# One block of rows, and one product per token tile, for two groups of remainder channels in the X accumulation of a layer's backward pass

## The chip, the cores and the metric

The kernel runs on one core of a Trainium2 chip. The metric is the time of one execution on the device in microseconds. Three runs of the kernel before took 1150.02, 1150.79 and 1152.15 us; their median is 1150.79 us. The engines are named as in the profile: PE (TensorE's products), PEld (its weight loads), DVE (VectorE), ACT (ScalarE), POOL (GpSimd) and SP (SyncE, whose queue issues nearly all DMAs).

## The reference

The program computes a layer's output and all its gradients. The layer has a global branch (self-attention over T = 4000 tokens, one head of D = 144 channels) and a local branch (a gated convolution of width 5), both fed from the layer norm of x; a second convolution and a product merge them. B is 2.

```python
xa = _layernorm(x)
q, k, v = split(xa @ w_qkv)
p = softmax(q @ k.T * D ** -0.5)
glob = (p @ v) @ w_att_out
h = gelu(xa @ w_mlp_in)                 # 2 D channels
u, g = h[..., :D], _layernorm(h[..., D:])
loc = (u * conv5(g, dw_csgu)) @ w_mlp_out
m = concat(glob, loc)
out = x + (m + conv5(m, dw_merge)) @ w_merge
# and the gradients of x and of the seven weights for a given grad_out
```

The gradient with respect to xa is what matters here. It has three parts for a token: one from the keys and values (sums over all query tiles), one from the queries, and one from the local branch's first product, whose input gradient has 2 D = 288 channels.

## The kernel before

Tokens are laid out as 125 partitions by 32 blocks per batch, so a token tile is 125 tokens, and there are 64 tiles in two batches. A channel dimension of 144 is one block of 128 and a remainder of 16; the 288 channels of the inner gradient are two blocks of 128 and a remainder of 32.

`phase_att` walks through 64 query tiles in steps. In step s it computes, for 32 key blocks at a time, the scores of tile s (`quad`, lines 1187 and 1194), their row minimum (`S_min`, 1209), exponentials (`P_exp`, 1215), and the product of probabilities and their gradient (`PdP`, 1225 and 1226). The results lie in Pbuf and Sbuf; DMA transposes issued by SP turn them into PT and ST (1219 and 1405). `Y_half` (1236) multiplies PT with xa, `Z_half` (1266) ST with xa. Y gives the row sums, the scalars rl, delta and nd (1242 to 1245), and yn, a copy for later (1247) that goes to memory (1248). Z becomes a row zn of 144 channels (1270): the query part of the gradient before its weight M1T. zn lies in columns 512 to 767 of a buffer qb, whose first 512 columns hold the q rows of a later tile; one DMA transpose per tile (`jit_tr`, 1165) turns all of it, so Z's transposed form is two blocks of 128: channels 0 to 127, and the 16 remaining with zeros behind them.

`X_group` adds up the gradient of xa in PSUM for up to three token blocks (1322) and adds it to acc in SBUF (1329). For each block its products are: one from Sbuf and one from Pbuf for every query tile of the group; two with M1T from Z's transposed blocks; and three with WiT from the inner gradient's blocks. The latter come from `local_units`: the local branch runs in 16 pairs of tiles per batch beside attention, `e_dh` writes the inner gradient into dhr (687), columns 0 to 287 of 384, and `dhT_unit` has it transposed (691).

The order of the instructions on each engine is not the program's: `Planner.ORDER` holds one list for each of PE, DVE, ACT, POOL and SP, and `plan` ties each instruction to the one before it in the list. SP's list orders the DMA issues. POOL has mostly the addition that makes the second row of QBs (1256), the powers for the layer norms (600), l_w (681) and additions to accumulators (698).

Before the loop, `Head` makes the weights of the products: `m1t` M1T, `conv` WiT by transposing w_mlp_in on PE and copying on ACT (298 to 301). After it, `Merge` and `Final` compute the outputs.

Of the kernel before, what the change touches and what calls it, by code (L numbers as in the profile page):

```python
# [120 lines left out]
class Head:  # L121
# [84 lines left out]

    def m1t(self):
        self.fused(self.WkT, self.WqT, float(D) ** -0.5, self.W.M1T)
# [81 lines left out]
    def conv(self):  # L290
# [10 lines left out]
        nc.scalar.copy(W.WiT[0:32, 2, :], pt[0:32, 2, :])  # L301
        nc.sync.dma_start(W.Wc[:, 0, :], k.dw_csgu.rearrange("k c -> (k c)").partition_broadcast(128))
# [35 lines left out]
def pre_pieces(k, W, b, S, pst):  # L338
# [4 lines left out]
    if True:  # L343
# [20 lines left out]
        def ln_mv(g):  # L364
# [9 lines left out]
            nc.gpsimd.tensor_tensor(S.rstd_x[:, sl], veps[:, sl], k.mhalf[0:PB, sl], op=ALU.pow)  # L374
# [42 lines left out]
def prep_late(k, W, b, S, es, pst):  # L417
# [7 lines left out]
    st = one([PB, NB, 6], F32, "pst")  # L425
# [26 lines left out]
    def stats(g):  # L452
        sl = slice(8 * g, 8 * g + 8)
        for j in range(8):
            nc.vector.bn_stats(st[:, 8 * g + j, :], xin[:, 8 * g + j, :])
        ma, mb, va, vb = st[:, sl, 1], st[:, sl, 4], st[:, sl, 2], st[:, sl, 5]
        nc.vector.tensor_tensor(dm[:, sl], ma, mb, op=ALU.subtract)
        nc.vector.tensor_tensor(sm[:, sl], ma, mb, op=ALU.add)
        nc.vector.tensor_tensor(veps[:, sl], va, vb, op=ALU.add)
        nc.vector.scalar_tensor_tensor(dm[:, sl], dm[:, sl], 0.25 * D, dm[:, sl], op0=ALU.mult, op1=ALU.mult)  # L460
        nc.vector.tensor_tensor(veps[:, sl], veps[:, sl], dm[:, sl], op=ALU.add)
        nc.vector.tensor_scalar(veps[:, sl], veps[:, sl], 1.0 / D, EPS, op0=ALU.mult, op1=ALU.add)
        nc.gpsimd.tensor_tensor(S.rstd_x[:, sl], veps[:, sl], k.mhalf[0:PB, sl], op=ALU.pow)
# [53 lines left out]

G2 = 2
# [5 lines left out]
def local_units(k, W, b, S, A, es, DHT, ps_w, gw):  # L524
# [6 lines left out]
    sm = es.enter_context(tc.tile_pool(name="loc_sm%d" % b, bufs=4, side=side, reuse_waits="tile"))  # L531
# [30 lines left out]
    def slot(g):  # L562
        return g % 3
# [119 lines left out]
    def e_dh(g):  # L683
# [3 lines left out]
        nc.vector.tensor_tensor(dhr[g % 2][0:PB, :, 0:2 * D], dd[:], gpr[slot(g)][:], op=ALU.mult)  # L687

    def dhT_unit(g):
        dhT = gw.tile([128, 3 * G2, 128], BF, tag="dhT", bufs=3)  # L690
        nc.sync.dma_start_transpose(out=dhT[:], in_=dhr[g % 2][:].rearrange("p a b -> p (a b)"))
        for bi in range(G2):
            DHT[G2 * g + bi] = [dhT[:, 3 * bi + ct, :] for ct in range(3)]
# [82 lines left out]
class Planner:  # L776

    ORDER = {
# [1414 lines left out]
```

## Time and profile before

| | us |
|---|---|
| median of three runs | 1150.79 |
| profiled execution | 1152.39 |
| its span | 1150.5 |
| PE busy in the span | 1118.8 |
| DVE busy | 1021.0 |
| ACT busy | 906.5 |
| POOL busy | 249.5 |

A row of a group gives line, engine, operation, the tile written and those read, the shapes and the count; then busy us, mean ns of one instruction, idle time of the engine just before, and what ended it. Successive matmuls overlap, so their mean duration is longer than their spacing. A row of the timeline gives start, length, engine, line, operation and tiles; for SP it is the issue of a DMA, not its landing. SPq, ACTq and so on are the engines' sequencers.

### The profile page before, as it was taken

The page shows a single profiled execution, that of the slowest core. Times are in us where ns is not written, and L with a number is a line of the kernel's source. Part 1 is how long each engine was busy: PE and PEld are TensorE (multiplying, and loading weights), DVE is VectorE, ACT ScalarE, POOL GpSimd, SP SyncE. Part 2 cuts the span into 40 slices and gives each one's busy share as a digit, 9 for nine tenths or more (in the row PEclk, how much of TensorE's full clock was granted, in tenths as well). Part 3 has the DMA queues.
Part 4 walks back from the last instruction along what each step waited for, and adds up shares of the span by engine and source line. Part 5 has one row for each costly group of instructions (what it writes and reads, how often), then busy time and mean ns, then how long its engine had stood idle before and what let it go on. Part 6 is the DMA issues. An engine that isn't in the chain of part 4 may idle for free.

```text
span 1150.5 us, 35851 instructions
## 1 busy us (share of the span) xinstructions
PE 1118.8 (97%) x14293; PEld 868.7 (76%) x14293; DVE 1021.0 (89%) x3063; ACT 906.5 (79%) x1641; POOL 249.5 (22%) x427
## 2 busy tenths in 40 slices
PE   6999999999999999999999999999999999999998
PEld 3667777777777677777777777777777777699987
DVE  8699999999999998877999999999999997667656
ACT  5999898899898767777989889888889877615372
POOL 8111112111121113431001111111111112013642
PEclk9999999999999999999999999999999999999999
DMA  4688887979988989998988989888888899978973
GB/s 117 155 160 176 173 181 158 192 159 173 174 166 159 188 181 182 201 187 183 207 183 178 171 158 168 161 181 152 173 174 154 187 177 183 224 173 219 245 144 101
DMA packets 680887, 200.72 MB, mean 174 GB/s; under 512 B 657815, under 2 KB 674093, under 8 KB 680699
## 3 DMA queue, kind: packets, MB, share of 16 engines
q1 hardware_dynamic: 678352, 194.69, 84.6%
q0 software_dynamic: 2192, 3.62, 1.1%
q8 instruction: 111, 1.82, 0.7%
q14 instruction: 56, 0.46, 0.1%
q10 hardware_dynamic: 176, 0.12, 0.0%
HBM read 24.62 MB, written 18.01 MB: 37 GB/s over the span
## 4 chain that ended last, share of the span: by engine, by line
PE 64%; DMA 13%; DVE 11%; ACT 7%; issue 2%; SPq 1%; POOL 1%; ACTq 0%; DVEq 0%; POOLq 0%
PE X L1322 18%; PE ps L1187 14%; PE yz L1236 8%; PE yz L1266 8%; PE ps L1194 5%; DMA PT<-Pbuf 5%; DVE Pbuf L1209 4%; ACT Pbuf L1215 3%; PE po L1708 2%; DMA ST<-Sbuf 2%; PE pd L610 1%; DVE Sbuf L1226 1%; PE pj L1147 1%; ACT Sbuf L1225 1%; DMA go_h<-in_grad_out_dram 1%
## 5 line engine op out<-in xcount | busy, mean ns | idle before, releaser
L1209 DVE TENSOR_SCALAR_CACHE_REDUCE Pbuf<-ps 125x1000 bf16<-125x1000 f32 x256 | 306.2, 1197 | 30.1 <-PE ps L1194 22.4
L1225 ACT CAST Sbuf<-ps 125x1000 bf16<-125x1000 f32 x249 | 248.7, 999 | 86.7 <-PE ps L1194 66.2
L1215 ACT ACTIVATE Pbuf<-Pbuf,nm 125x1000 bf16<-125x1000 bf16 x256 | 284.9, 1144 | 4.4 <-DVE nm L1211 4.2
L1322 PE MATMUL X<-QBs,Pbuf 125*128 125x144 bf16 x2048 | 281.1, 226 | 0.2 <-POOL QBs L1256 0.2
L1322 PE MATMUL X<-QBs,Sbuf 125*128 125x144 bf16 x2048 | 281.3, 226 | 0.0
L1187 PE MATMUL ps<-xaT_m,qt 128*128 128x500 bf16 x1024 | 260.6, 374 | 5.0 <-DVE Pbuf L1209 3.5
L1322 PEld LDWEIGHTS <-Sbuf 125*128 125x128 bf16 x2048 | 198.2, 98 | 18.8 <-issue 18.5
L1322 PEld LDWEIGHTS <-Pbuf 125*128 125x128 bf16 x2048 | 200.2, 98 | 1.3 <-issue 1.1
L1226 DVE TENSOR_TENSOR Sbuf<-Sbuf,Pbuf 125x1024 bf16<-125x1024 bf16 x249 | 170.8, 690 | 7.9 <-ACT Sbuf L1225 6.0
L1236 PE MATMUL yz<-xa_aug,PT 125*128 125x145 bf16 x2048 | 151.0, 227 | 6.5 <-DMA PT<-Pbuf 6.4
L1266 PE MATMUL yz<-xa_aug,ST 125*128 125x144 bf16 x2048 | 150.8, 228 | 3.6 <-DMA ST<-Sbuf 2.4
L1236 PEld LDWEIGHTS <-PT 125*128 125x128 bf16 x2048 | 130.7, 98 | 21.6 <-DMA PT<-Pbuf 10.5
L1187 PEld LDWEIGHTS <-qt 128*128 128x128 bf16 x1024 | 91.4, 97 | 68.6 <-issue 7.0
L1266 PEld LDWEIGHTS <-ST 125*128 125x128 bf16 x2048 | 132.9, 98 | 12.2 <-issue 7.1
L1329 DVE TENSOR_TENSOR acc<-X,acc 125x432 f32<-125x432 f32 (+1 forms) x204 | 109.8, 548 | 15.3 <-PE X L1322 14.8
L1256 POOL TENSOR_TENSOR QBs<-g,g 125x144 bf16<-125x144 f32 x64 | 35.2, 550 | 379.2 <-ACT g L1255 290.9
L1194 PEld LDWEIGHTS <-qt 16*128 16x128 bf16 x1024 | 26.3, 91 | 108.9 <-issue 108.9
L1194 PE MATMUL ps<-XR,qt 16*128 16x500 bf16 x1016 | 100.4, 380 | 0.0
L681 POOL TENSOR_SCALAR l_w<-ring,nc,c 125x144 f32<-125x144 bf16 x64 | 31.8, 504 | 167.0 <-DVE nc L677 122.4
L653 DVE TENSOR_TENSOR l_prod<-ring,Wc 125x720 bf16<-125x720 bf16 x128 | 65.9, 535 | 0.2
L1611 PE MATMUL Hps<-Yg,go_h 125*128 125x144 bf16 x640 | 54.3, 226 | 0.0
L600 POOL TENSOR_TENSOR rsr<-ve,mhalf 125x2 f32<-125x2 f32 x32 | 25.4, 795 | 126.9 <-DVE ve L599 107.4
(540 smaller groups left out, 1946.4 us busy)
## 6 DMA issues: line engine op xcount, KB each, us to landing
Yn_d<-yn SPq DMA_DIRECT2D x64, 36.0 KB
Zn_d<-qb SPq DMA_DIRECT2D x64, 36.0 KB
ug_d<-ugr SPq DMA_DIRECT2D x32, 72.0 KB
Yg<-Yn_d SPq DMA_DIRECT2D x8, 288.0 KB
Yg<-ug_d SPq DMA_DIRECT2D x8, 288.0 KB
Zn<-Zn_d SPq DMA_DIRECT2D x4, 576.0 KB
PT<-Pbuf SPq DMA_TRANSPOSE x128
ST<-Sbuf SPq DMA_TRANSPOSE x128
```

The lines of the kernel that those rows point to most:

```text
L653: nc.vector.tensor_tensor(prod[:, bi].rearrange("p a b -> p (a b)"), ring[:, a, p + bi:p + bi + 5, :].rearrange("p a b -> p (a b)"), W.Wc[ ...
L1187: mm = nc.tensor.matmul(pp[r // 2][:, r % 2, 0:CH], QT[i][:, 2 * h, :], bs(i)[0].xaT_m[:, c * CH:(c + 1) * CH], start=True, stop=False)
L1194: nc.tensor.matmul(pp[r // 2][:, r % 2, 0:CH], QT[i][rs, 2 * h + 1, :], xr, start=False, stop=True)
L1209: nc.vector.tensor_scalar(pv(pc(i, c2)), src, -1.0, 3.0e38, op0=ALU.mult, op1=ALU.min, accum_out=NM[i][:, c2:c2 + 1])
L1215: nc.scalar.activation(v, v, ACT.Exp, bias=NM[i][:, 4:5], scale=-1.0)
L1225: nc.scalar.copy(pv(sc(i, c2)), src)
L1226: nc.vector.tensor_tensor(sc(i, c2), sc(i, c2), pc(i, c2), op=ALU.mult)
L1236: nc.tensor.matmul(Yw, PT[0:PB, pos(i, j), :], S.xa_aug[:, j, 0:D + 1], start=(j == 0), stop=(j == NB - 1))
L1266: nc.tensor.matmul(Zw, ST[0:PB, j, :], S.xa_aug[:, j, 0:D], start=(j == 0), stop=(j == NB - 1))
L1322: nc.tensor.matmul(X[:, jj, :], l, r, start=(n_ == 0), stop=(n_ == len(ops) - 1))
L1329: nc.vector.tensor_tensor(av, X[0:PB, 0:nj, :], av, op=ALU.add)
L1611: nc.tensor.matmul(H[0:rows, a // 3, (a % 3) * D:(a % 3 + 1) * D], lhs, self.src[b][h][:, 2 + j, :], start=(n == 0 and a % 3 == 0), stop=( ...
```

## The change

The last 16 channels of Z and the last 32 of the inner gradient are put into one transposed block, and the weights that belong to them into the matching rows of one weight block, so that one product takes both. Which block it is depends on which of the two is there first in program order. A small tile, `rest`, with eight places for a tile's remainder, carries it over:

- Where Z comes first, its 16 channels are copied to `rest`, and from there into columns 288 to 303 of dhr's row. Z then takes one product and the inner gradient three; the third block of WiT gets M1T's last 16 rows at rows 32 to 47 (`m1t_rem`).
- Where the inner gradient comes first, its 32 channels are copied to `rest`, and from there into columns 160 to 191 of zn. The inner gradient then takes two products and Z two; the second block of M1T gets WiT's last 32 rows at rows 32 to 63.

The copies are on POOL, the new weights in `conv`. To make room, mhalf shrinks from 48 to 8 columns, the prep's statistics from 32 to 8 places, a pool of small tiles from four buffers to three, and the scratch tile dj goes: the product that makes delta writes its elementwise output into yn, where the copy of Y follows. All five lists of `Planner.ORDER` are new.

```diff
+    def m1t_rem(self, dst):
+        nc, pt = self.k.nc, self.ps([128, D], F32)
+        for kt in range(2):
+            nc.tensor.matmul(pt[0:48, :], self.WkT[:, kt, 96:D], self.WqT[:, kt, :], start=(kt == 0), stop=(kt == 1))
+        nc.scalar.activation(dst, pt[32:48, :], ACT.Copy, scale=float(D) ** -0.5)
...
         nc.scalar.copy(W.WiT[0:32, 2, :], pt[0:32, 2, :])
+        p2 = self.ps([128, D], BF)
+        nc.tensor.transpose(p2[0:64, 0:128], Wi[:, 0, 224:288], ident[:])
+        nc.tensor.transpose(p2[0:64, 128:D], self.Wi2[:, 224:288], ident[0:DR, 0:DR])
+        nc.scalar.copy(W.M1T[32:64, 1, :], p2[32:64, :])
+        self.m1t_rem(W.WiT[32:48, 2, :])
...
-    st = one([PB, NB, 6], F32, "pst")
+    st = one([PB, 8, 6], F32, "pst")
...
+class Rest:
+
+    def __init__(self, nc, pool):
+        self.nc, self.n = nc, 8
+        self.d = pool.tile([PB, self.n, 2 * DR], BF, name="rest")
+        self.zd, self.dd, self.open = ([set(), set()] for _ in range(3))
+        self.live = {}
+
+    def late(self, b, j):
+        return j in self.open[b]
...
+    def outer(self, b, j, zn):
+        q = j % self.n
+        if j in self.dd[b]:
+            assert self.live.pop(q) == (b, j)
+            self.nc.gpsimd.tensor_copy(zn[0:PB, 160:192], self.d[:, q, :])
+        else:
+            self.put(b, j)
+            self.nc.gpsimd.tensor_copy(self.d[:, q, 0:DR], zn[0:PB, 128:D])
+        self.zd[b].add(j)
+
+    def inner(self, b, j0, dh):
+        early = [j in self.zd[b] for j in (j0, j0 + 1)]
+        for w in (True, False):
+            bi = [q for q in range(2) if early[q] == w]
+            if not bi:
+                continue
+            a, n = bi[0], len(bi)
+            q = (j0 + a) % self.n
...
+            if w:
+                self.nc.gpsimd.tensor_copy(dh[0:PB, a:a + n, 288:304], self.d[:, q:q + n, 0:DR])
+            else:
+                self.nc.gpsimd.tensor_copy(self.d[:, q:q + n, :], dh[0:PB, a:a + n, 256:288])
...
-    sm = es.enter_context(tc.tile_pool(name="loc_sm%d" % b, bufs=4, side=side, reuse_waits="tile"))
+    sm = es.enter_context(tc.tile_pool(name="loc_sm%d" % b, bufs=3, side=side, reuse_waits="tile"))
...
         nc.vector.tensor_tensor(dhr[g % 2][0:PB, :, 0:2 * D], dd[:], gpr[slot(g)][:], op=ALU.mult)
+        k.rest.inner(b, G2 * g, dhr[g % 2])
...
-            DHT[G2 * g + bi] = [dhT[:, 3 * bi + ct, :] for ct in range(3)]
+            DHT[G2 * g + bi] = [dhT[:, 3 * bi + ct, :] for ct in range(3 - k.rest.late(b, G2 * g + bi))]
...
-    k.mhalf = small.tile([128, 48], F32, name="mhalf")
+    k.rest = Rest(nc, small)
+    k.mhalf = small.tile([128, 8], F32, name="mhalf")
...
-        dj = small.tile([PB, D], BF, tag="dj", bufs=1)
-        nc.vector.scalar_tensor_tensor(dj[:], Y[:, 0:D], rl, qb[:, 1, 0:D], op0=ALU.mult, op1=ALU.mult, accum_out=delta)
+        yn = ynr[i % 2]
+        nc.vector.scalar_tensor_tensor(yn[0:PB], Y[:, 0:D], rl, qb[:, 1, 0:D], op0=ALU.mult, op1=ALU.mult, accum_out=delta)
         nc.vector.scalar_tensor_tensor(nd, delta, -1.0, rl, op0=ALU.mult, op1=ALU.mult)
-        yn = ynr[i % 2]
         nc.scalar.activation(yn[0:PB], Y[:, 0:D], ACT.Copy, scale=rl)
...
+        k.rest.outer(i // NB, i % NB, zn)
         ZN[i] = zn
...
-                ops += [(zt[:, q, :], W.M1T[:, q, :]) for q in range(2)]
+                ops += [(zt[:, q, :], W.M1T[:, q, :]) for q in range(1 + k.rest.late(b, j))]
```

In `Planner.ORDER` the lists begin as follows (DVE and SP have as many entries as before, 2521 and 826; PE has 1379 in place of 1385 runs, ACT 1644 in place of 1642, POOL 526 in place of 423):

```diff
-        "PE": [36, 37, 38, 39, 40, 41, 0, 1, 42, 2, 3, 4, 5, 43, 6, 7, 8, 44, 9, 10, 11, 53, 12, 45, 13, 46, 14, 47, 15, 16, 17, 48, 18, 54, 19, 49,
+        "PE": [36, 37, 38, 39, 40, 41, 0, 1, 42, 2, 3, 4, 5, 43, 6, 7, 8, 9, 44, 10, 11, 12, 13, 53, 14, 45, 15, 46, 16, 47, 17, 18, 54, 19, 48, 20,
...
-        "SP": [0, 1, 4, 3, 19, 2, 30, 5, 6, 9, 16, 21, 44, 10, 7, 45, 13, 18, 27, 39, 22, 46, 40, 60, 14, 12, 15, 23, 11, 8, 25, 31, 26, 28, 32, 20,
+        "SP": [0, 1, 2, 13, 9, 3, 5, 30, 4, 10, 7, 23, 39, 6, 16, 27, 42, 11, 43, 14, 19, 29, 41, 15, 12, 26, 24, 20, 22, 47, 8, 31, 46, 32, 25, 21,
```

More of the change, by code (lines that the diff above doesn't have):

```diff
@@ L373, in ln_mv @@
             nc.vector.tensor_scalar(veps[:, sl], veps[:, sl], 1.0 / D, EPS, op0=ALU.mult, op1=ALU.add)
-            nc.gpsimd.tensor_tensor(S.rstd_x[:, sl], veps[:, sl], k.mhalf[0:PB, sl], op=ALU.pow)
+            nc.gpsimd.tensor_tensor(S.rstd_x[:, sl], veps[:, sl], k.mhalf[0:PB, :], op=ALU.pow)
         def ln_nm(g):
@@ L454, in stats @@
         for j in range(8):
-            nc.vector.bn_stats(st[:, 8 * g + j, :], xin[:, 8 * g + j, :])
-        ma, mb, va, vb = st[:, sl, 1], st[:, sl, 4], st[:, sl, 2], st[:, sl, 5]
+            nc.vector.bn_stats(st[:, j, :], xin[:, 8 * g + j, :])
+        ma, mb, va, vb = st[:, :, 1], st[:, :, 4], st[:, :, 2], st[:, :, 5]
         nc.vector.tensor_tensor(dm[:, sl], ma, mb, op=ALU.subtract)
@@ L462, in stats @@
         nc.vector.tensor_scalar(veps[:, sl], veps[:, sl], 1.0 / D, EPS, op0=ALU.mult, op1=ALU.add)
-        nc.gpsimd.tensor_tensor(S.rstd_x[:, sl], veps[:, sl], k.mhalf[0:PB, sl], op=ALU.pow)
+        nc.gpsimd.tensor_tensor(S.rstd_x[:, sl], veps[:, sl], k.mhalf[0:PB, :], op=ALU.pow)
     def norm(g):
@@ L515, in prep_late, with put @@
     return P
+class Rest:
[6 more added lines that the diff above has]
+        return j in self.open[b]
+    def put(self, b, j):
+        assert self.live.get(j % self.n) is None
+        self.live[j % self.n] = (b, j)
+    def outer(self, b, j, zn):
[15 more added lines that the diff above has]
+            q = (j0 + a) % self.n
+            for x in bi:
+                self.dd[b].add(j0 + x)
+                if w:
+                    assert self.live.pop((j0 + x) % self.n) == (b, j0 + x)
+                else:
+                    self.open[b].add(j0 + x)
+                    self.put(b, j0 + x)
+            if w:
+                self.nc.gpsimd.tensor_copy(dh[0:PB, a:a + n, 288:304], self.d[:, q:q + n, 0:DR])
+            else:
+                self.nc.gpsimd.tensor_copy(self.d[:, q:q + n, :], dh[0:PB, a:a + n, 256:288])
 G2 = 2
@@ L778 @@
     ORDER = {
[53 rows of a table removed]
-        "DVE": [0, 2, 1, 3, 4, 10, 5, 11, 9, 8, 6, 7, 12, 14, 15, 13, 16, 17, 40, 43, 25, 18, 44, 20, 22, 23, 19, 32, 24, 21, 34, 33, 35, 36, 26, 28,
[98 rows of a table removed]
[53 rows of a table added]
+        "DVE": [2, 0, 3, 1, 4, 5, 7, 11, 10, 6, 9, 8, 12, 14, 15, 16, 13, 17, 22, 24, 21, 23, 20, 19, 42, 37, 18, 32, 41, 34, 25, 33, 35, 36, 26, 28,
[98 rows of a table added]
             2411, 2458, 2409, 2463, 2464, 2418, 2465, 2466, 2410, 2467, 2468, 2469, 2470, 2471, 2457, 2472, 2420, 2461, 2419, 2460, 2474, 2473, 2475,
@@ L934 @@
             2509, 2517, 2510, 2511, 2512, 2518, 2519, 2520],
-        "Activation": [1, 0, 4, 5, 2, 3, 7, 6, 8, 9, 10, 13, 29, 32, 14, 15, 11, 33, 16, 17, 18, 12, 37, 35, 34, 19, 20, 21, 24, 22, 23, 31, 27, 26,
[64 rows of a table removed]
-        "Pool": [8, 5, 15, 4, 11, 0, 12, 10, 1, 3, 47, 7, 2, 16, 18, 6, 19, 17, 41, 25, 26, 24, 50, 33, 32, 31, 9, 53, 37, 38, 20, 30, 42, 23, 13,
[43 rows of a table removed]
+        "Activation": [1, 0, 4, 2, 5, 3, 6, 10, 11, 7, 29, 8, 9, 33, 13, 14, 15, 30, 12, 37, 16, 34, 18, 17, 23, 19, 20, 24, 36, 21, 32, 27, 22, 26,
[64 rows of a table added]
+        "Pool": [0, 1, 15, 7, 8, 3, 9, 6, 2, 4, 16, 5, 19, 18, 10, 11, 17, 14, 26, 25, 24, 41, 32, 33, 31, 37, 268, 38, 20, 23, 27, 22, 21, 28, 35,
[47 rows of a table added]
             805, 788, 813, 761, 821, 771, 789, 798, 804, 820, 797, 807, 822, 823, 814, 808, 806, 824, 825, 815],
```

516 rows, old and new, of the table ORDER are left out of this document.

## The prediction

> **What bounds the kernel now.** I read the page's first parts, then the busy times of the stretch in which X is accumulated, then the chain that ended last and the waits. Of the page:
>
> ```profile
> span 1150.5 us, 35851 instructions
> PE 1118.8 (97%) x14293; PEld 868.7 (76%) x14293; DVE 1021.0 (89%) x3063; ACT 906.5 (79%) x1641; POOL 249.5 (22%) x427
> PEclk9999999999999999999999999999999999999999
> PE 64%; DMA 13%; DVE 11%; ACT 7%; issue 2%; SPq 1%; POOL 1%; ACTq 0%; DVEq 0%; POOLq 0%
> ```
>
> TensorE's clock is full throughout, so its work can be counted at one rate. The stretch from the first product of X to the last, and four stretches of 50 us of which two stand here with their mean (columns: stretch, length, then busy us of PE, PEld, DVE, ACT, POOL, granted clock, DMA share, GB/s):
>
> ```profile
> 51.80:1031.60 979.80, 964.19 (x12131) 733.89 (x12130) 902.54 (x2588) 809.38 (x1419) 167.99 (x281) 1.00 0.90 177
> 200.00:250.00 50.00, 50.00 (x638) 38.30 (x637) 49.11 (x147) 45.77 (x80) 9.27 (x16) 1.00 0.84 168
> 600.00:650.00 50.00, 49.94 (x635) 38.11 (x633) 49.14 (x146) 44.27 (x83) 8.76 (x13) 1.00 0.90 172
> sum 200.00, PE 199.00 PEld 150.92 DVE 196.84 ACT 171.42 POOL 34.02; mean PE 49.75 PEld 37.73 DVE 49.21 ACT 42.85 POOL 8.51
> ```
>
> In 979.8 us PE is idle for 15.6 us. Where the local work runs beside attention, PE is busy 99.5% and DVE 98.4%: PE is the bound, with DVE one per cent behind it. POOL has 812 us free. Who waits for whom, of the waits:
>
> ```profile
> PE yz L1236 <- DMA PT<-Pbuf: 6.4, 11, 1.0
> PE ps L1187 <- DVE Pbuf L1209: 3.5, 12, 0.9
> PE yz L1266 <- DMA ST<-Sbuf: 2.4, 3, 1.2
> DVE Pbuf L1209 <- PE ps L1194: 22.4, 46, 1.7
> DVE acc L1329 <- PE X L1322: 14.8, 21, 1.8
> ```
>
> DVE waits for PE 37.2 us in two rows, PE for DVE 3.5 us: a shorter PE is passed on. PE's other waits are for the DMA transposes that SP issues.
>
> **Term 1: products of X.** The groups of lines by form, the rows of tile M1T (shortest, median and longest ns, first and last start), and one piece of the chain (start, length, what):
>
> ```profile
> L1322 PE MATMUL X<-WiT,dhT 128*128 128x144 bf16 x192 | 21.7, 226 | 0.0
> L1322 PE MATMUL X<-M1T,qt 128*128 128x144 bf16 x128 | 19.0, 226 | 0.0
> L1322 PE MATMUL X<-M1T,qt x128: 223/227/237, 80.4 to 1031.6; 128*128 128x144 bf16 x128
> 95.73 3.00 PE X L1322 x48
> ```
>
> The 320 products of Z and of the inner gradient become 256: in program order the gradient comes first for 27 tiles (2 + 2 products) and Z first for 37 (1 + 3), four a tile either way. The mean of 226 ns is a latency; in a row 48 products take 3.00 us, 62.5 ns each. So 64 x 62.5 ns = **-4.0 us** of PE, all of it within the bound stretch. The transposing DMAs keep their sizes, and the additions into acc their count, so only PE becomes shorter.
>
> **Term 2: the head.** conv gains two transposes and two 144-column products (about 4 x 62.5 ns = 0.25 us of PE) and two ScalarE copies. Rows of the like:
>
> ```profile
> L301 ACT COPY WiT<-hps x1: 252/252/252, 49.8 to 49.8; 32x144 bf16<-32x144 bf16 x1
> L182 ACT ACTIVATE M1T<-hps x2: 275/290/306, 36.6 to 37.9; 128x144 bf16<-128x144 f32 x1, 16x144 bf16<-16x144 f32 x1
> ```
>
> 0.25 + 0.29 us on ACT, and two more turns of the three PSUM tiles. Between 0 and 0.8 us if both engines' shares add; PE's own share is certain, so I take **+0.3**. M1T's first reader comes 30 us later (80.4 us), so nothing waits for the new weights.
>
> **Term 3: 103 copies on POOL** (64 behind Z, 39 behind the 32 gradient pairs, seven of which are split). The nearest rows, and the pair of DVE lines that meets POOL most:
>
> ```profile
> L495 POOL COPY pstrip<-xa_aug 125x64 bf16<-125x64 bf16 x8 | 1.9, 237 | 4.0 <-DVE xa_aug L470 4.0
> L653 DVE TENSOR_TENSOR l_prod<-ring,Wc x128: 508/526/924, 91.2 to 946.2; 125x720 bf16<-125x720 bf16 x128
> L653 DVE TENSOR_TENSOR l_prod<-ring,Wc 125x720 bf16<-125x720 bf16 x128 | 65.9, 535 | 0.2
> L1226 DVE TENSOR_TENSOR Sbuf<-Sbuf,Pbuf x249: 657/684/1056, 43.8 to 1016.5; 125x1024 bf16<-125x1024 bf16 x125
> L1226 DVE TENSOR_TENSOR Sbuf<-Sbuf,Pbuf 125x1024 bf16<-125x1024 bf16 x249 | 170.8, 690 | 7.9 <-ACT Sbuf L1225 6.0 <-ACT Pbuf L1215 1.6
> 273.77 1.65 POOL L698 TENSOR_TENSOR A_dWiT<-l_fl,A_dWiT 128x432 f32<-128x432 f32 x1 [4.71 <-PE yz L1236]
> 274.89 0.92 DVE L653 TENSOR_TENSOR l_prod<-ring,Wc 125x720 bf16<-125x720 bf16 x1
> ```
>
> 103 x 0.237 = 24.4 us of POOL, hidden in its 812 free ones. What can show is DVE held up by POOL, as at 274.89 us: 0.92 us in place of 0.526. Mean less median gives what this costs today: 128 x 9 ns + 249 x 6 ns = 2.6 us beside 168 us of POOL work; 24.4 us more at that rate are 0.4 us of DVE. Bounds 0 and 24.4 us (every copy holds DVE for its whole length; DVE has 77 us idle in the stretch). I take **+0.2** on the path. The Trainium skill's page "SBUF — State Buffer", section "Who interferes with whom", says that a DVE instruction with two SBUF inputs and a GpSimd one that reads SBUF exclude each other, the later one waiting in full; the rows agree in kind, and by that rule alone the sum could lose up to the upper bound, which the 2.6 us of today speaks against.
>
> Z's copy itself stands before the transpose of the next q rows but two. The tightest of 60 distances:
>
> ```profile
> 874.46 0.37 DVE L1270 SCALAR_TENSOR_TENSOR qb<-yz,nm,ty 125x144 bf16<-125x144 f32 x1
> 880.86 1.75 SPq L1165 DMA_TRANSPOSE qt<-qb  x1
> ```
>
> 6.0 us, which hides a copy of 0.24 us: 0.
>
> **Term 4: yn as the scratch output of delta.** The write to yn now starts on DVE, which must wait for the store of Yn two tiles earlier; ACT had that wait before.
>
> ```profile
> L1247 ACT ACTIVATE yn<-yz,nm 125x144 bf16<-125x144 f32 x64 | 24.4, 381 | 9.2 <-DVE dj L1244 5.8 <-DMA Yn_d<-yn 2.7 <-PE pw L723 0.4
> 133.48 0.58 SPq L1248 DMA_DIRECT2D Yn_d<-yn  x1
> 134.91 0.36 DVE L1244 SCALAR_TENSOR_TENSOR dj<-yz,nm,qb 125x144 bf16<-125x144 f32 x1
> 135.75 0.38 ACT L1247 ACTIVATE yn<-yz,nm 125x144 bf16<-125x144 f32 x1 [2.09 <-DMA Yn_d<-yn]
> ```
>
> The store landed 2.27 us after its issue, where DVE came after 1.43: it would have waited 0.84 us, with nd, the new row minimum and the next S_min behind it. ACT waits so twice, 2.7 us; bounds 0 and 2.7. Setting the new lists against the old times, only two of 62 pairs stand closer than 3 us. I take **+0.2**.
>
> mhalf, st and the smaller ring of three keep their instructions and readers: 0.
>
> **Term 5: the new order.** All five lists are rewritten; by count 133 of SP's 826 places and 485 of DVE's 2521 hold the same entry as before, DVE's entries moving 3.4 places on average. It does not say which way. It can at best take away the 15.6 us of PE idle time, and could as well double it; half of that, +-8 us, is what I keep for the range, and 0 in the sum, since both lists serve the same loops with the same two or three near-equal engines.
>
> **Sum:** -4.0 + 0.3 + 0.2 + 0.2 = -3.3 us. The profiled execution took 1152.39 us (1150.5 of span, 1.9 around it) and would take 1149.1. The three runs shown have a median of 1150.79, 1.6 lower, and by that measure I predict **1147.5 us**.
>
> **Rivals.**
>
> *Slower, by SP's queue.* The gradient's copy goes between DVE's L687 and the transpose L691, which is issued in order with PT and ST.
>
> ```profile
> 662.72 0.45 DVE L687 TENSOR_TENSOR dhr<-l_dd,gpr 125x576 bf16<-125x576 bf16 x1
> 663.20 1.21 SPq L691 DMA_TRANSPOSE dhT<-dhr  x1
> 664.34 0.50 POOL L1256 TENSOR_TENSOR QBs<-g,g 125x144 bf16<-125x144 f32 x1 [8.65 <-ACT g L1255]
> 664.50 2.35 SPq L1405 DMA_TRANSPOSE ST<-Sbuf  x1
> 209.93 0.45 DVE L687 TENSOR_TENSOR dhr<-l_dd,gpr 125x576 bf16<-125x576 bf16 x1
> 211.61 1.22 SPq L691 DMA_TRANSPOSE dhT<-dhr  x1
> POOL QBs L1256 <- ACT g L1255: 290.9, 43, 17.9
> ```
>
> Six of the 32 transposes are issued within 1.23 us of L687's end, from 0.03 (663.20) to 1.23 (211.61). Were the copy queued behind the L1256 that waits for ACT until 664.34, it would end at 664.84 + 0.24 = 665.08, and L691 with the ST transpose behind it would come 1.9 us later. ST and PT feed the rows in which PE waits. At 1.9 us a case two cases eat the gain, and from three on (5.7 - 3.3 = +2.4) the kernel is slower; with six it loses 11.4 and stands at 1159, with four, 1155. For it: POOL's QBs waits up to 17.9 us for ACT. Against: the new list can put the copy ahead of that addition or the transpose later; mostly it does not stand behind one. Chance 0.25, other losses of the new order through the same queue included.
>
> *No change, DVE is the bound.* At 98.4% DVE might set the pace, and PE's 4 us turn into idle time before L1187: 1150.8. Against it are the 37.2 us in which DVE waits for PE. Chance 0.13.
>
> *No change, PE isn't full.* PEld is busy for 734 of 980 us; if that were the measure, 246 us would be free and 64 products would fit in anyway: 1150.8. Against it: 48 products in 3.00 us without a gap. Chance 0.05. The Trainium skill's "Perfetto Trace Analysis", section "Identifying the Most-Contended Engine", does take the weight loads' busy share in place of the matmuls'; here the start-to-start spacing decides.
>
> *Faster by more.* The new order also takes half of PE's idle time: 1147.5 - 7.8 = 1139.7. Nothing speaks for it but that the list was made anew. Chance 0.10.
>
> **Numbers.** The forecast case has the rest, 0.47, with a range of its own from 1145 to 1148.4. About 0.2% (2.3 us) is what a measurement of this kernel can tell from no change. Faster 0.47 + 0.10 = 0.57, within it 0.18, slower 0.25. The range takes in the nearer part of the better order's case and the slower rival to its four cases, 1155, and a little beyond: 1141 to 1156, which leaves out about 0.05 below and 0.1 above.
>
> **What would show it.** X's products: 4352 in place of 4416, still 62.5 ns apart, and PE's busy time in the stretch about 4 us lower with its idle time near 15.6 us. POOL some 24 us busier, L653 and L1226 with the same medians. A DVE wait for the Yn store under 2 us in all. The forecast is wrong if PE's idle time grows by more than 4 us: before L1236 and L1266 it would be SP's queue, before L1187 DVE.

## The result and the profile after

The changed kernel takes **1161.51 us** (median of four runs, 1161.25 to 1163.38) against 1150.55 for the kernel before on the same chip: a ratio of **1.0094**, 95% interval 1.0079 to 1.0110. It became slower by 11 us; 3.3 us less was forecast. The profiled execution took 1161.54 us, its span is 1159.8 (before 1150.5).

The page of the changed kernel (helpers and loop stand some 60 lines lower in it: L1322 of before is L1385, L1236 L1299, L1187 L1250, L691 L749, L1737 L1800):

```profile
span 1159.8 us, 35845 instructions
PE 1116.9 (96%) x14233; PEld 865.9 (75%) x14233; DVE 1016.9 (88%) x3063; ACT 906.7 (78%) x1643; POOL 276.6 (24%) x530
```

The busy times of the stretch from the first product of X to the last, of two pieces in its middle, and of the first 980.2 us of that stretch (there PE had 964.59 before):

```profile
51.74:1034.20 982.46, 961.25 (x12067) 730.39 (x12066) 898.26 (x2585) 808.62 (x1419) 194.88 (x384) 1.00 0.90 176
200.00:250.00 50.00, 49.99 (x635) 38.16 (x634) 48.97 (x150) 45.31 (x81) 10.18 (x22) 1.00 0.95 178
600.00:650.00 50.00, 50.00 (x629) 37.68 (x628) 48.79 (x147) 45.00 (x83) 10.01 (x19) 1.00 0.84 168
51.80:1032.00 980.20, 958.99 (x12031) 728.13 (x12029) 897.65 (x2584) 808.28 (x1419) 193.97 (x382) 1.00 0.90 176
```

From the first product of X to the last, PE has 64 instructions fewer (12067 for 12131) and 2.9 us less to do (961.25 for 964.19), but it is idle for 21.2 us where it was idle for 15.6. The products went as described; their groups, and behind them the waits that the prediction named, are these:

```profile
L1385 PE MATMUL X<-WiT,dhT 128*128 128x144 bf16 x165 | 19.6, 225 | 0.0
L1385 PE MATMUL X<-M1T,qt 128*128 128x144 bf16 x91 | 16.2, 226 | 0.0
```

```profile
PE yz L1299 <- DMA PT<-Pbuf: 9.7, 12, 1.5
PE yz L1328 <- DMA ST<-Sbuf: 2.3, 4, 0.8
PE ps L1250 <- DVE Pbuf L1272: 3.4, 12, 0.9
```

SyncE's own waits for POOL ahead of the gradient's transpose:

```profile
SPq L749 <- POOL QBs L1318: 5.4, 7, 1.2
```

165 + 91 = 256 products, 64 fewer. PE's wait for PT grew by 3.3 us; its wait for DVE did not grow.

Where the 9.3 us of span went was read by setting equal milestones of the two traces against each other (the starts of the row minimum, the writes of Z, the products of the output stage): at the last Z, 1028 us, the changed kernel is 1.5 us behind, where the forecast had it 3.3 ahead; among the first products of the output stage it goes from 2.5 us behind (1062 us of before) to 11.1 (1074 us), and it ends 9.3 behind. So about 5 us are missing in the loop and 8 behind it, where the diff leaves the program as it was and only the order is new. These figures come from one trace of each kernel; the runs with exchanged tails, below, say the same with medians. From 1035 to 1125 us, the waits of before and then of the changed kernel:

```profile
DVE t L1734 <- POOL dxo L1737: 12.4, 5, 3.8
POOL dxo L1737 <- DMA out_dram<-dxo: 6.0, 2, 5.0
```

```profile
DVE t L1797 <- POOL dxo L1800: 20.1, 7, 5.0
POOL dxo L1800 <- DMA out_dram<-dxo: 14.8, 4, 4.5
```

POOL waits longer for the store that frees its output buffer, DVE for POOL.

### The profile page after: what moved, and what is told of

It reads as the page before. It is cut to its first block, busy times and chain, and to the rows that moved or that the text cites. A ratio compares the mean times of both kernels' runs of the same rounds, so it can differ in the third digit from the quotient of the medians.

```text
span 1159.8 us, 35845 instructions
## 1 busy us (share of the span) xinstructions
PE 1116.9 (96%) x14233; PEld 865.9 (75%) x14233; DVE 1016.9 (88%) x3063; ACT 906.7 (78%) x1643; POOL 276.6 (24%) x530
## 3 DMA queue, kind: packets, MB, share of 16 engines
q8 instruction: 111, 1.82, 0.7%
## 4 chain that ended last, share of the span: by engine, by line
PE 68%; DMA 12%; DVE 10%; ACT 5%; issue 3%; POOL 2%; SPq 1%; ACTq 0%; POOLq 0%; DVEq 0%
PE X L1385 17%; PE ps L1250 14%; PE yz L1299 9%; PE yz L1328 8%; PE ps L1257 5%; DMA PT<-Pbuf 5%; DMA ST<-Sbuf 3%; DVE Pbuf L1272 3%; PE Hps L1674 3%; PE po L1771 2%; ACT Pbuf L1278 2%; DMA out_dram<-dxo 2%; PE pd L667 1%; PE pj L1210 1%; DVE Sbuf L1289 1%
## 5 line engine op out<-in xcount | busy, mean ns | idle before, releaser
L1385 PE MATMUL X<-QBs,Pbuf 125*128 125x144 bf16 x2048 | 281.7, 226 | 1.9 <-POOL QBs L1318 1.8
L1385 PE MATMUL X<-QBs,Sbuf 125*128 125x144 bf16 x2048 | 282.0, 226 | 0.0
L1250 PE MATMUL ps<-xaT_m,qt 128*128 128x500 bf16 x1024 | 260.5, 374 | 4.0 <-DVE Pbuf L1272 3.4
L1385 PEld LDWEIGHTS <-Sbuf 125*128 125x128 bf16 x2048 | 198.3, 98 | 20.5 <-issue 20.2
L1385 PEld LDWEIGHTS <-Pbuf 125*128 125x128 bf16 x2048 | 200.2, 98 | 0.3
L1299 PE MATMUL yz<-xa_aug,PT 125*128 125x145 bf16 x2048 | 150.8, 227 | 10.6 <-DMA PT<-Pbuf 9.7
L1299 PEld LDWEIGHTS <-PT 125*128 125x128 bf16 x2048 | 130.8, 98 | 25.7 <-DMA PT<-Pbuf 13.7
L1250 PEld LDWEIGHTS <-qt 128*128 128x128 bf16 x1024 | 91.5, 97 | 67.0 <-issue 6.7
L1318 POOL TENSOR_TENSOR QBs<-g,g 125x144 bf16<-125x144 f32 x64 | 38.0, 594 | 359.8 <-ACT g L1317 300.7
L1798 ACT ACTIVATE t<-t,dx_c,rstd_x 125x144 f32<-125x144 f32 x64 | 29.6, 501 | 37.1 <-DVE t L1797 25.8
```

The lines of the kernel that those rows point to most:

```text
L1250: mm = nc.tensor.matmul(pp[r // 2][:, r % 2, 0:CH], QT[i][:, 2 * h, :], bs(i)[0].xaT_m[:, c * CH:(c + 1) * CH], start=True, stop=False)
L1299: nc.tensor.matmul(Yw, PT[0:PB, pos(i, j), :], S.xa_aug[:, j, 0:D + 1], start=(j == 0), stop=(j == NB - 1))
L1385: nc.tensor.matmul(X[:, jj, :], l, r, start=(n_ == 0), stop=(n_ == len(ops) - 1))
```

## The experiments

Every ratio is against the kernel before on the same chip, with its 95% interval.

### Change and order apart, loop and tail apart

Two runs of the changed kernel and two of the kernel before, with the lists or parts of them exchanged. An entry keeps its neighbours; "tail" is all that starts behind 1031 us in the trace of the kernel whose loop is used.

```diff
-    ORDER = {new lists}, st of 8 places
+    ORDER = {lists of before, each copy where its input was ready}, st of 16 places
```

> The change with the five lists of before, the 103 copies put in at the times at which their inputs were ready in the trace of before. Two adaptations: the prep's statistics have 16 places in place of 8, and one store of Yn stands five places earlier in SP's list, since with the old lists the new write to yn would wait for it for ever. Theory A (the new lists cost the time, the change itself is worth what the sum said): 1150.6 - 3.3 = 1147.3 us. Theory B (the change's copies, weights and waits cost the time, whatever the lists): near 1161 us.

Measured: 1173.76 us, 1.0199 (1.0172 to 1.0227). Neither theory holds. The change in the old order costs 23 us; the profiled execution is 20.1 behind at the last Z and 20.2 at its end, so all of it lies in the loop. A part of it is TensorE's clock: in stretches of 50 us the granted clock of this trace is 0.97 from 400 and from 550 us and 0.93 from 900 us, 1.00 in all others up to 1150 us, which makes at most 6.5 us. The last of the three holds a wait of PE of 4.2 us for PT. In the trace of before and in that of the changed kernel it is 0.99 or 1.00 everywhere.

```diff
 (kernel before)
-    ORDER = {lists of before}
+    ORDER = {new lists without the copies}
```

> The program of before, with the five lists of the changed kernel less its new entries; runs of X's products are cut so that the products stand in the same places. Theory A: the lists carry all the loss and the 64 products are back, so 1161.5 + 3.3 = 1164.8 us. Theory B: as before, 1150.6 us.

Measured: 1165.43, 1.0118 (1.0084 to 1.0151). The new order costs 14 us by itself.

```diff
 (changed kernel)
-    ORDER = {new loop, new tail}
+    ORDER = {new loop, tail of before}
```

> The changed kernel; what starts before 1031 us in its trace keeps its lists, and all that follows stands in the relative order of before. At 1028 us the changed kernel is 1.5 us late, at the end 9.3. Theory A1 (most of the loss is in the order behind the X loop): 1161.5 - 7.8 = 1153.7 us. Theory A2 (the loop's lists leave a state that makes the end late, whatever its order): near 1161 us.

Measured: 1153.92, 1.0018 (1.0004 to 1.0031).

```diff
 (kernel before)
-    ORDER = {loop of before, tail of before}
+    ORDER = {loop of before, new tail}
```

> The kernel before; what starts before 1031 us in its trace keeps its lists, and all that follows stands in the relative order of the changed kernel. Theory A1: 1150.6 + 7.8 = 1158.4 us. Theory A2: 1150.6 us.

Measured: 1157.06, 1.0050 (1.0027 to 1.0072). Given and taken away, the new order of the tail costs 8.7 us (0.0094 - 0.0018) and 5.8 us. What is left, +0.18% or 2.1 us, is the changed loop, with its 64 products fewer; 3.3 us less was forecast.

### What 64 products are worth

```diff
-                ops += [(zt[:, q, :], W.M1T[:, q, :]) for q in range(2)]
+                ops += [(zt[:, q, :], W.M1T[:, q, :]) for q in range(1)]
```

> The kernel before with its five lists, from which only the second product of Z is left out in each of the 64 token tiles (64 products of 62.5 ns; the gradient's three products, the copies and the buffers stay as before). It leaves out the part of x's gradient that comes from Z's 16 remainder channels. Theory A, the prediction's term 1 (TensorE bounds the stretch, a shorter TensorE is passed on): 4.0 us less than the kernel before, 1146.6. Theory B (the stretch is paced by the loop through TensorE, VectorE, SyncE's transposes and back, and TensorE's idle time only grows): within 1.5 us of the kernel before. Theory C (what TensorE executes is loaded as code in blocks of 16384 bytes, one per 128 products, and a SyncE issue during which such a block is loaded takes 0.5 to 1.6 us more; with 64 products fewer the blocks fall half a block later by the end of the stretch and hit other transposes): off by several us in either direction, most likely 3 to 15 us slower, in steps of 1 to 5 us at a PT or ST transpose whose issue has become long.

Measured: 1162.41, **1.0110** (1.0094 to 1.0126). Less work for TensorE and nothing else, in the old lists, and 12.6 us slower: only theory C allows for that. It came from the traces: SyncE has 622 DMA issues between 52 and 1030 us of before, 69 of which take over 0.5 us more than the median of their line. In 51 of these 69 a block of 16384 bytes on the instruction queue starts during the issue or at most 0.3 us ahead of it, in the other 553 in 31; if the 94 blocks fell anywhere, the lengths of the issues would give 18 and 73. The next two runs test it with the work untouched.

```diff
-        for _ in range(n):
-            nc.tensor.matmul(pt[:], z[:, 0:128], z[:], start=True, stop=True)
+        for i in range(n + 64):
+            w = 8 if i < 64 else 256
+            nc.tensor.matmul(pt[:, 0:w], z[:, 0:128], z[:, 0:w], start=True, stop=True)
```

> The kernel before, the whole of its work and its lists, with 64 more dummy products of 8 columns on zeros ahead of TensorE's first instruction, where TensorE is idle (its first instruction starts at 6.29 us, the zeros are written at 1.43 us). 64 products are half a block of code, so that each later block of TensorE's code is loaded about 4 to 5 us earlier against the work than before. Theory C (position of the code blocks against SyncE's transposes decides): the loop's time changes by more than 2 us, slower more likely than faster, 1153 to 1165, with other SyncE issues long than before. Theory B or A (the position does not matter): the loop as before, in all 1150.6 to 1152 (at most a little later at the start).

Measured: 1166.29, **1.0145** (1.0128 to 1.0162).

> As the kernel with half a block, but with 128 dummy products, a whole block of code (90 ahead of the first instruction, 12 and 26 in two gaps of the first 10 us). The later blocks are then loaded where they were before. Theory C: the loop runs as before, its milestones shifted by one constant, the delay at the start (0 to 5 us): total 1150.6 to 1155.6, and less different from before within the loop than the half block. If half a block and a whole block come out alike, or differ only by their delay at the start, theory C falls.

With 128 in place of 64 in the same lines. Measured: 1149.56, **1.0009** (0.9993 to 1.0026). Half a block costs 17 us, a whole one nothing. The dummies themselves lie in idle time ahead of TensorE's first transpose at 6.42 us, as the trace of the half block shows:

```profile
1.65 1.87 PE L193 MATMUL warm<-wz 128*128 128x8 bf16 x64 [1.65 <-DVE wz L189]
```

SyncE's issues at one place, of before and then of the half block:

```profile
133.48 0.58 SPq L1248 DMA_DIRECT2D Yn_d<-yn  x1
136.58 2.08 SPq L691 DMA_TRANSPOSE dhT<-dhr  x1
141.77 1.61 SPq L1405 DMA_TRANSPOSE ST<-Sbuf  x1
```

```profile
133.43 1.71 SPq L1247 DMA_DIRECT2D Yn_d<-yn  x1
138.13 1.21 SPq L692 DMA_TRANSPOSE dhT<-dhr  x1
142.44 2.89 SPq L1404 DMA_TRANSPOSE ST<-Sbuf  x1
```

Where before a block started at 136.40 us and the gradient's transpose was long, it is short now, and the store and the ST transpose are long instead, with blocks at 133.39 and 143.60. PE's waits for PT and ST rose from 6.4 and 2.4 us:

```profile
PE yz L1235 <- DMA PT<-Pbuf: 9.1, 13, 1.5
PE yz L1265 <- DMA ST<-Sbuf: 5.2, 7, 1.3
```

The DMA view of 133.3 to 135.2 us (GB/s in 40 slices, then the queues), of before and of the half block:

```profile
GB/s 286 286 296 280 291 291 286 296 264 291 291 243 296 286 275 253 291 269 280 307 264 291 307 264 296 296 248 233 238 293 200 100 82 48 30 18 6 0 0 0
q1 hardware_dynamic: 1678, 0.42, 98.9%
```

```profile
GB/s 135 539 259 275 275 264 275 275 269 269 280 183 22 16 22 16 16 0 0 0 0 0 0 0 0 0 0 0 0 0 5 5 11 11 5 11 5 11 11 11
q1 hardware_dynamic: 581, 0.15, 145.8%
q8 instruction: 1, 0.02, 4.5%
```

With a block on q8, the core's other transfers fall to almost nothing about half a microsecond after its start and stay down for more than a microsecond. (The fall at the end of before's row has no block near it.) Over the 94 blocks of the stretch in before, other packets start at 38 per quarter microsecond 1.5 us behind a block's start, against 164 on average. The Trainium skill's "Runtime: NRT & Kernel Launch", section "Instruction fetch mechanics", says that code comes in blocks of 16 KiB, 256 instructions, and that crossing a block's end is mostly hidden. The traces agree on the size (1.82 MB in 111 packets on q8); TensorE itself was idle for only 15.6 us in a stretch with 94 blocks, but the transfers beside it are held up.

Three more positions, with 32, 96 and 8 in the same lines:

> The kernel before with 32 dummy products ahead of TensorE's first instruction, a quarter of a block of code. Theory C: the loop is another one than before, with a total between before and the half block (1150 to 1167), not within 1 us of before. Rival: it is the delay or the warmth of TensorE at the start, not the position of the code, that made the 17 us of the half block; then 32 give about half of them, 1158, and a whole block should have given 34 and did not; so for the rival nothing is left but chance, and 32 come out at 1150.

Measured: 1158.37, 1.0066 (1.0044 to 1.0087).

> The kernel before with 96 dummy products (90 ahead of the first instruction, 6 in the first gap), three quarters of a block. Theory C: as with a quarter, 1150 to 1167, with the blocks a quarter of their distance later than before in place of earlier; a total within 1 us of before at a quarter and at three quarters alike would speak against the theory.

Measured: 1167.14, 1.0145 (1.0122 to 1.0168).

> The kernel before with 8 dummy products ahead of TensorE's first instruction, a sixteenth of a block (32 cost 7.6 us, 96 cost 16.7). Theory C: between no change and a few us, 1148 to 1154, with most of the issues hit that are hit before; it is also the one try for a position of the code that suits the order of before better than its own.

Measured: 1149.56, 0.9997 (0.9986 to 1.0007). So by the position, from none to a whole block: 0, 0 (a sixteenth), 7.6, 17, 17 and 1 us. None of the positions tried was measurably better than that of before. The cost comes back to nothing after one block, as it would for the place of the blocks and not for a delay. For the changed kernel with the old tail, the half block:

> The changed kernel with the order of before behind the loop (1153.92 in the run with the old tail), with the same 64 dummy products ahead of TensorE's first instruction. Theory C: the loop changes by more than 2 us in either direction against the kernel with the old tail, 1145 to 1165. Theory A or B: 1153.9 to 1155.

Measured: 1170.04, 1.0175 (1.0157 to 1.0194), 18 us above the same kernel without the dummies by the ratios. The new loop, too, loses at another position of the code; one was tried. Then the products' own worth, with the code kept in place:

```diff
-                ops += [(zt[:, q, :], W.M1T[:, q, :]) for q in range(2)]
+                ops += [(zt[:, 0, :], W.M1T[:, 0, :]), (zt[:, 1, :], W.M1T[:, 1, 0:8])]
...
-                nc.tensor.matmul(X[:, jj, :], l, r, start=(n_ == 0), stop=(n_ == len(ops) - 1))
+                w = r.shape[-1]
+                nc.tensor.matmul(X[:, jj, 0:w], l, r, start=(n_ == 0), stop=(n_ == len(ops) - 1))
```

> The kernel before with its lists; Z's second product keeps its place in TensorE's code in all 64 token tiles and is cut from 144 to 8 columns (29 ns apart in the row of dummy products, 1.87 us for 64, in place of 62.5 ns). It leaves out the part of x's gradient that Z's 16 remainder channels give, but for 8 columns. TensorE then has 64 x 33.5 ns = 2.1 us less to do, and its blocks of code are loaded at the same instructions as before. Theory A (term 1 with the code kept in place: a shorter TensorE is passed on): 2.1 us less than before. Theory B (the stretch is paced by the loop through TensorE, VectorE and SyncE): no change within 1 us. Theory C (where the code is loaded decides) says only that the 12.6 us lost by leaving the products out must be gone: within 3 us of before in either direction.

Measured: 1147.99, **0.9981** (0.9970 to 0.9992): 2.2 us less (0.9 to 3.5), where 2.1 were worked out. A shorter TensorE is passed on. All weight loads are still there, so the gain also speaks against the rival that counts by them.

### The copies and yn

The changed kernel in the order of before, with short products on zeros in the places of those that it saves:

```diff
-WARM = 36
+WARM = 32
...
-                ops += [(zt[:, q, :], W.M1T[:, q, :]) for q in range(1 + k.rest.late(b, j))]
+                late = k.rest.late(b, j)
+                ops += [(zt[:, q, :], W.M1T[:, q, :]) for q in range(1 + late)] + ([] if late else [(zt[64:128, 0, :], W.M1T[64:128, 1, 0:8])])
...
+                if ct == 1 and k.rest.late(b, j):
+                    ops.append((a[64:128], W.M1T[64:128, 1, 0:8]))
```

> The whole change with the order of before (as in the run with the old order, 1173.76), and in the place of each of the 64 removed products a product of 8 columns with zeros, four dummy products at the start taken away for the four that the head gains: TensorE's code has the length that it had before at every point. Theory C: the 21.6 us that the run with the old order lost against its kernel before mostly go, 1148 to 1154; what stays above before minus 2.1 us is the price of the copies and of yn as scratch. If the copies on POOL or the new wait of VectorE for the store of Yn cost the 21.6 us (theory D), it stays above 1160.

Measured: 1168.72, 1.0165 (1.0144 to 1.0185). The padding gave back 0.34% of 1.99, and the two intervals overlap; the total stays above 1160, as theory D had it. So theory C explains at most the smaller part of this loss. One of its steps is the prediction's slower rival, here POOL and then SyncE of that kernel (8.9 us behind before at this point):

```profile
901.67 0.21 POOL L552 COPY rest<-qb 125x16 bf16<-125x16 bf16 x1 [1.88 <-DVE qb L1329]
901.94 0.54 POOL L571 COPY dhr<-rest 125x16 bf16<-125x16 bf16 x1
```

```profile
894.92 1.61 SPq L1279 DMA_TRANSPOSE PT<-Pbuf  x1
902.51 1.21 SPq L750 DMA_TRANSPOSE dhT<-dhr  x1
903.82 1.62 SPq L1279 DMA_TRANSPOSE PT<-Pbuf  x1
```

The old order has the gradient's rows ready first, but the block's roles are fixed by the program: the gradient's copy stands behind Z's, which waits for qb. In before L691 was issued at 887.77, here at 902.51, 5.8 us later than 887.77 + 8.9; PT with it. The new order has no place of that size: its seven waits of the transpose for POOL take 5.4 us in all. The other steps of this run were not traced to one cause, and the run doesn't separate the copies' work from the places that they got in the old lists.

```diff
 (kernel before)
-        dj = small.tile([PB, D], BF, tag="dj", bufs=1)
-        nc.vector.scalar_tensor_tensor(dj[:], Y[:, 0:D], rl, ...
+        yn = ynr[i % 2]
+        nc.vector.scalar_tensor_tensor(yn[0:PB], Y[:, 0:D], rl, ...
```

> The kernel before with its lists; of the change only the scratch output of delta goes to yn in place of dj (one store of Yn stands five places earlier in SyncE's list, without which the lists would block each other). Term 4 of the prediction: 0 to 2.7 us, +0.2 taken, so 1150 to 1151. If VectorE's new wait for the store of Yn makes the 14.9 us by which the loop with the padded change ended later than before (theory D1), 1160 or more. Between, 1152 to 1158: D1 makes a part of it.

Measured: 1153.32, 1.0036 (1.0021 to 1.0051), 4.1 us. In its trace DVE's new wait is small:

```profile
DVE yn L1239 <- DMA Yn_d<-yn: 1.3, 3, 0.7
```

The profiled execution (1151.84 us, the fastest of the twelve) shows no loss, so where the median's 4 us lie stays open.

```diff
 (kernel before, new lists without the copies)
+LATE = [the 17 and 10 token tiles of the changed kernel whose gradient comes first]
-                ops += [(zt[:, q, :], W.M1T[:, q, :]) for q in range(2)]
+                ops += [(zt[:, q, :], W.M1T[:, q, :]) for q in range(1 + (j in LATE[b]))]
-            DHT[G2 * g + bi] = [dhT[:, 3 * bi + ct, :] for ct in range(3)]
+            DHT[G2 * g + bi] = [dhT[:, 3 * bi + ct, :] for ct in range(3 - (G2 * g + bi in LATE[b]))]
```

> The five new lists on a kernel that has TensorE's products exactly as the changed one (Z's second product left out in 37 token tiles, the gradient's third in 27; four dummies at the start for the four that the head gains, so that the code has the changed kernel's length throughout), but none of the 103 copies, and dj in place of yn. It leaves out the remainder channels of Z or of the gradient in each tile's part of x's gradient. If the copies and yn as scratch cost nothing in the order made for them, it takes what the changed kernel takes, 1161 to 1162; if they cost what yn alone cost in the old order (4.1 us), 1157; if they make the whole loss, 1148 to 1151. Theory C: well below the new lists on the kernel before with its longer code (1165.43), since those lists now meet the code where they met it in the changed kernel.

Measured: 1162.43, 1.0102 (1.0084 to 1.0121). Without copies and without yn it is as slow as the changed kernel: in their own order they cost nothing that can be measured, and the loss is there without them. It goes with the new order and the code that it meets, and these two do not simply add up: the old order with 64 products left out lost as much (1.0110). The run is not well below the run of the new lists with the longer code (1.0118), as theory C had it: between these two the position of the code decides little.

### Which list behind the loop

The changed kernel with the tail of before in POOL's list alone, in SyncE's alone, and in all but POOL's:

```diff
-        "Pool": [new loop, new tail]
+        "Pool": [new loop, tail of before]
```

> The changed kernel; of POOL's list alone the part behind the loop (what starts after 1031 us) is in the order of before, the other four lists are the new ones. If POOL's order of stores and weight loads makes the loss behind the loop (theory P), it takes what the run with all five old tails took, 1154 to 1156. If SyncE's, VectorE's, ScalarE's or TensorE's order makes it, 1160 to 1162.

Measured: 1160.94, 1.0101 (1.0083 to 1.0119). In its trace the wait seen above is mostly gone, VectorE waiting 5.3 us for POOL's dxo in place of 20.1, but TensorE has a new one:

```profile
PE Hps L1670 <- POOL go_r L1651: 6.2, 1, 6.2
```

```diff
-        "SP": [new loop, new tail]
+        "SP": [new loop, tail of before]
```

> The changed kernel; of SyncE's list alone the part behind the loop is in the order of before. Theory P (POOL's order makes the loss there): 1160 to 1162. If SyncE's order makes it: 1154 to 1156.

Measured: 1159.97, 1.0085 (1.0066 to 1.0104).

```diff
-        "PE", "DVE", "Activation", "SP": [new loop, new tail]
+        "PE", "DVE", "Activation", "SP": [new loop, tail of before]
```

> The changed kernel with the order of before behind the loop in the lists of TensorE, VectorE, ScalarE and SyncE, and POOL's list new throughout. If POOL's order does no harm there (the runs with only POOL's or only SyncE's old tail came out at 1160.9 and 1160.0), 1153 to 1155, as with all five old. If POOL's order is one of two causes that each suffice, 1159 to 1162.

Measured: 1170.08, 1.0174 (1.0154 to 1.0195), 9 us more than with five new tails. Its trace has one long wait of TensorE, and behind it a lower granted clock (the last column but two), which was 1.00 here in the changed kernel:

```profile
PE po L1767 <- DVE xo L1770: 6.7, 1, 6.7
1050.00:1100.00 50.00, 43.32 (x642) 42.97 (x640) 27.62 (x123) 17.84 (x37) 24.65 (x44) 0.90 0.79 205
1100.00:1150.00 50.00, 47.56 (x710) 43.92 (x709) 28.76 (x141) 27.98 (x70) 22.26 (x32) 0.93 0.48 121
```

So POOL's old tail alone gives nothing back, nor does SyncE's, and theory P is not borne out. But a mixed tail brings long waits of its own, so these three runs don't say which list costs the 8 us of the tail; TensorE's, VectorE's and ScalarE's were not exchanged alone. The 8 us are shown for the five lists together; which arrangement in them costs it stays open.

## Why the prediction was wrong

- **Term 5, the new order at 0, is the step that failed.** The reason given, that both lists serve the same loops, does not make them equal. On the unchanged program the new lists cost 1.18%, 14 us; with the change the total is +0.94%, and +1.02% without its copies and yn. About 8 of the 14 us between forecast and result lie behind the loop (8.7 us with only the tail's order exchanged), where the prediction did not look at all: its bound of 8 us was made from PE's idle time in the loop. Some 5 us more are in the loop, by PE's idle time (15.6 to 21.2 us, ahead of L1299 for 3.3 of them). What the order and what the shifted code has of these 5 was not separated.
- **Term 1, -4.0 us: the price was right, and so was the claim that PE bounds the stretch** (2.2 us for 2.1 worked out, with the products shortened in their places). What failed is "so only PE becomes shorter": taking products away also moves TensorE's code, and in the old order 64 products fewer cost 12.6 us where 4.0 less was worked out. In the changed kernel PE is busy 2.9 us less from the first product of X to the last, and the idle time takes it up.
- **Term 2, the head, +0.3:** the first product of X starts at 51.7 us in both traces, within 0.2 us; nothing speaks against it.
- **Term 3, the copies:** right on the path. POOL has 27.1 us more (24 expected), and DVE's medians stayed (525 and 683 ns for 526 and 684); their means:

```profile
L710 DVE TENSOR_TENSOR l_prod<-ring,Wc 125x720 bf16<-125x720 bf16 x128 | 65.7, 533 | 0.4 <-POOL ring L681 0.2
L1289 DVE TENSOR_TENSOR Sbuf<-Sbuf,Pbuf 125x1024 bf16<-125x1024 bf16 x249 | 171.1, 692 | 2.1 <-ACT Pbuf L1278 1.0 <-ACT Sbuf L1288 1.0
L551 POOL COPY rest<-qb 125x16 bf16<-125x16 bf16 x37 | 11.1, 306 | 40.7 <-DVE qb L1332 37.9 <-DVE c L736 2.8
```

  The upper bound, every copy holding DVE for its whole length, was 24.4 us; 533 and 692 ns on average, against 535 and 690, show next to none of it.
- **Term 4, yn, +0.2 of at most 2.7:** in the old order 4.1 us (2.4 to 5.9) by the median, so probably above the bound; in the new order nothing that can be measured, and no wait of DVE for the store of Yn is in its trace.
- **The rivals.** The slower one had the right queue and, for this kernel, not the cause that cost the time: SyncE's waits for POOL's QBs ahead of the gradient's transpose occur, seven of them, but are at most 1.2 us long in place of 1.9, 5.4 us in all, and no wait of PE for PT or ST comes within 20 us behind one. In the old order the case exists, at 5.8 us. The two without change fall with the run of short products.
- The sign to look for was named: PE's idle time up by more than 4 us, ahead of L1236. It rose by 5.6, 3.3 of it there; for the 8 us behind the loop the prediction named no sign.

## What to carry over

A change that alters the number of TensorE's instructions in a kernel with a written-out order is two changes: the work, and the place of every later block of code against the transfers. Separate them with dummy products in idle time at the start or with short products in the old places, before the change itself is judged. And price a new order by its own run, in every stage that it rewrites, not only where the change is.

## What the runs showed of the hardware that was not expected

- TensorE's code comes in packets of 16384 bytes, 111 for 14293 products and their weight loads, about one per 128 products. Behind a packet's start the core's other transfers fall, to a quarter of their mean rate at the lowest (38 for 164 packets per quarter microsecond), and of the 82 SyncE issues that one fell into, 51 took over 0.5 us more, of the 540 others 18. That this reaches PE through late transposes is read from the traces; that the position alone moves the time by up to 17 us of 1150 is shown by the runs with dummies.
- 64 products of 8 columns take 1.87 us, 29 ns each, where 48 of 144 columns in a row take 3.00 us, 62.5 ns each.
- A long wait of TensorE can cost twice: in the run with POOL's new tail among old ones TensorE waits 6.66 us, up to 1079.49, and the trace's clock record has 0.50 from 1075.23 to 1085.47 us. In the changed kernel a wait of 2.89 us, up to 1111.82, left it at 1.00. The trace of the half block has no stretch of 50 us below 1.00, so its loss does not need this.
